# Gated mix of two linear-attention blocks: stationary tiles of 128 columns in M, denominators between output-weight tiles, and A's last output product moved next to B's

## The chip, the cores and the metric

The kernel runs on one core of a Trainium2 chip. A core has five engines that run side by side and wait for one another through semaphores: TensorE (PE, matrix products, with a separate stream of weight loads, PEld), VectorE (DVE), ScalarE (ACT), GpSimd (POOL) and SyncE (SP, which here only issues DMAs). Products land in PSUM, eight banks of 128 partitions by 512 float32; everything else lives in SBUF. The metric is device time in microseconds (us) of one execution; lower is better.

## The reference

Inputs are x (2048 rows of 640), and for each of two branches A and B a weight wqkv (640 by 1920) and wo (640 by 640), all bf16; B's own x is not used. Each branch computes, with 32 heads of 20 columns:

```python
qkv = x @ wqkv                       # q, k, v: 2048 x 640 each
phi = lambda t: jnp.where(t > 0, t + 1, jnp.exp(t)) + 1e-6
pq, pk = phi(q), phi(k)
kv  = einsum("bhsd,bhse->bhde", pk, v)          # 20 x 20 per head
z   = einsum("bhsd->bhd", pk)
o   = einsum("bhqd,bhde->bhqe", pq, kv) / (einsum("bhqd,bhd->bhq", pq, z) + 1e-6)
branch = o @ wo
```

The output is g * A + (1 - g) * B, with one gate per row, g = sigmoid(sum(x * gate_w)).

## The kernel before

The work is reordered so that v is never formed. With pk the 2048 by 640 matrix of k features, G = x^T pk is 640 by 640; M = Wv^T G, of which only the diagonal blocks of the heads are needed, gives kv; WP = blockdiag(kv) wo is then a 640 by 640 weight, and the branch is (pq / den) WP. The order of the work is written out by hand: a small recording layer takes operations in program order, gives each engine its own list, and derives the semaphore waits from the tiles that operations read and write. Every engine runs its list strictly in that order.

The stages, in order of time:

- Transposes of x, the k products of all 16 row tiles of both branches with their feature maps (to about 48 us), then the q products and the G pieces of A mixed (to about 114 us). `g_piece` is one quarter of one 128-row strip of G: four row tiles, each a matmul of 512 and one of 128 moving columns.
- `m_part`: M in ten windows `w` of 80 columns of Wv by 64 columns of G (`W = 80`, `HS` the first head of each window). A window is five accumulating matmuls, stationary `WV[X][:, j, ds]` (128 rows by 80 columns), moving 64 columns of `GT`. Windows 0 to 7 go to one PSUM bank, 8 and 9 to another; VectorE then multiplies rows 0 to 79 by a mask of the head blocks into `MG`. One branch is 50 matmuls; both branches together are 100.
- `wp_tile`: one of five 128-row tiles `k` of WP. Each half (320 columns) is four matmuls that stand side by side in the array, with 32 stationary columns each, writing to partitions 32 g to 32 g + 31. ScalarE copies the first half out of PSUM, VectorE the second. The PSUM pairs of A's five tiles are 1, 2, 3, 1, 2 (pair p is banks 2p and 2p + 1).
- `den`: the denominators of one branch, 20 matmuls of 512 moving columns with 32 stationary columns, four side by side, into bank 6 (A) or 7 (B). VectorE adds EPS (L641), then takes reciprocals in four pieces for each branch (`recip`, L649). SP writes them to DRAM (`table`) and reads them back spread over the partitions (`widen`); VectorE multiplies the q features by them (`scale`, L684 and L692).
- `wp_a_den` issues A's five WP tiles, then A's and B's denominators, then reciprocals, tables and widened reads. It is hung into the G pieces of B: M of A stands after B's first G piece, `wp_a_den` after the second, and the other 18 pieces follow.
- `fin_mm(X, t)`: the output product of row tile t, five matmuls of 512 and five of 128 moving columns. `fin_a(t)` (ScalarE, L779) writes A's product times the gate to the float32 tile `TA[t % 5]`; `fin_out(t)` (VectorE, L796) adds B's product times one minus the gate, into `OSTG`, and a DMA writes it out. A's PSUM pairs are 2 and 1 by turns, B's 0 and 3. Between A's first output tiles stand M and the WP tiles of B.
- The closing loop runs over t = 0 to 15: A's tile t + 3 (for t from 1 to 12), then B's tile t. So the last products are A15, B12, B13, B14, B15. B's last tile is cut in three column pieces, 0 to 255, 256 to 479, 480 to 639, each in its own bank with its own VectorE instruction and its own DMA (ScalarE's queue for the first and third, SP's for the second).

Of the kernel before, what the change touches and what calls it, by code (L numbers as in the profile page):

```python
# [8 lines left out]
ACT = mybir.ActivationFunctionType  # L9
# [3 lines left out]
D = 640  # L13
H = 32
DH = 20
# [13 lines left out]
NW = 10  # L29
W = 80  # L30
HS = (0, 3, 6, 9, 12, 16, 19, 22, 25, 28)

C_MK = 0
C_ZM = 64 * NW
# [171 lines left out]
def bass_gated_mix__linear_attn_block__linear_attn_block__prompt_kernel(  # L206
# [18 lines left out]
    with ExitStack() as es:  # L225
        E = es.enter_context

        def sb(name, shape, dtype=dt.bfloat16):
            return E(nc.sbuf_tensor(name, shape, dtype))
# [7 lines left out]

        WK = {"A": sb("WKA", [128, NC, D]), "B": sb("WKB", [128, NC, D + 2])}
        WQ = {X: sb("WQ" + X, [128, NC, D]) for X in BR}
        WV = {X: sb("WV" + X, [128, NC, D]) for X in BR}  # L240
        PK = {X: sb("PK" + X, [128, NT, D]) for X in BR}
        PQ = {X: sb("PQ" + X, [128, NC, S]) for X in BR}
        WP = {X: sb("WP" + X, [128, NC, D]) for X in BR}
# [25 lines left out]
        def bank(i, lo, hi, p0=0, p1=128):  # L269
            o = 512 * (i % 2)  # L270
            return PP[i // 2][p0:p1, o + lo : o + hi]
# [38 lines left out]
        def act(fn, reads=(), writes=(), name=""):  # L310
            return sch.op("ACT", fn, reads=reads, writes=writes, name=name)
# [4 lines left out]
        def pool(fn, reads=(), writes=(), name=""):  # L316
            return sch.op("POOL", fn, reads=reads, writes=writes, name=name)
# [30 lines left out]
        def load_wk(eng, X, c0, c1):  # L348
# [19 lines left out]
            reads=[("ONE",)],  # L368
            writes=[("IDN",)],
        )  # L370
        act(
            lambda e: e.activation(SG[:, 2, 0:1], nc.const_aps.tensor(1.0, (128, 1), dt.float32), ACT.Exp),
            writes=[("SGE", 0)],
# [252 lines left out]
        def den(X, bk):  # L626
            xi = BR.index(X)
            steps = []
            for k in range(NC):
                for b in range(NB):  # L630
                    o = bank(bk, 0, 512, 32 * b, 32 * b + 32)
                    r = PQ[X][:, k, 512 * b : 512 * b + 512]
                    steps.append((o, ZBD[:, NC * xi + k, :], r, k == 0, k == NC - 1, (0, 32 * b)))
            mms(
                steps,
                reads=[("ZBD", X)] + [("PQ", X, b, k) for k in range(NC) for b in range(NB)],
                writes=[("PS", bk)],
                name="den%s" % X,
            )
            dve(  # L640
                lambda e: e.tensor_scalar(DT32[X][:, :], bank(bk, 0, 512), EPS, None, op0=ALU.add),  # L641
                reads=[("PS", bk)],
                writes=[("DT", X)],
            )
# [53 lines left out]
        def m_part(X, w0, w1, bk):  # L698
            n = w1 - w0
            steps = []  # L700
            for w in range(w0, w1):
                ds = slice(DH * HS[w], DH * HS[w] + W)
                steps += acc(
                    bank(bk, 64 * (w - w0), 64 * (w - w0) + 64, 0, W),
                    [(WV[X][:, j, ds], GT[:, j, 64 * w : 64 * w + 64]) for j in range(NC)],
                )
            mms(
                steps,
                reads=[("WV", X)] + [("GT", j) for j in range(NC)],
                writes=[("PS", bk)],  # L710
                name="m%s%d" % (X, w0),
            )
            dve(
                lambda e: e.tensor_tensor(
                    out=MG[:, w0:w1, :].rearrange("p w f -> p (w f)"),
                    in0=bank(bk, 0, 64 * n, 0, W),
                    in1=CB[0:W, C_MK + 64 * w0 : C_MK + 64 * w1],
                    op=ALU.mult,
                ),
                reads=[("PS", bk), ("CST",)],  # L720
                writes=[("MG", w) for w in range(w0, w1)],
            )

        def wp_tile(X, k, pp):
            P = PP[pp]
            cells = []
            for g in range(4):
                w = 8 + g // 2 if k == 4 else 4 * (k // 2) + g
                fs = slice(32 * (g % 2), 32 * (g % 2) + 32) if k == 4 else slice(k % 2, 64, 2)
                cells.append((w, MG[:, w, fs]))  # L730
            for j, (lo, hi) in enumerate(((0, D // 2), (D // 2, D))):
                mms(
                    [
                        (P[32 * g : 32 * g + 32, 512 * j : 512 * j + hi - lo], l, wo_at(X, w)[0][:, lo:hi], True, True, (0, 32 * g))
                        for g, (w, l) in enumerate(cells)
                    ],
                    reads=[("WO", X, w) for w, _ in cells] + [("MG", w) for w, _ in cells],
                    writes=[("PS", 2 * pp + j)],
                    name="wp%s%d" % (X, k),
                )  # L740
            for j, (lo, hi) in enumerate(((0, D // 2), (D // 2, D))):
                o, p = WP[X][:, k, lo:hi], P[:, 512 * j : 512 * j + hi - lo]
                (dve if j else act)(
                    lambda e, o=o, p=p, j=j: e.tensor_copy(o, p) if j else e.activation(o, p, ACT.Copy),
                    reads=[("PS", 2 * pp + j)],
                    writes=[("WP", X, k, j)],
                )
# [16 lines left out]
        def fin_mm(X, t):  # L764
            for lo, hi, bk in fin_split(X, t):
                mms(
                    acc(
                        bank(bk, 0, hi - lo),
                        [(PQ[X][:, k, 128 * t : 128 * t + 128], WP[X][:, k, lo:hi]) for k in range(NC)],
                    ),  # L770
                    reads=[("PQ", X, t // 4, k) for k in range(NC)] + [("WP", X, k, j) for k in range(NC) for j in (0, 1)],
                    writes=[("PS", bk)],
                    name="fin%s%d" % (X, t),
                )

        def fin_a(t):
            pp = fin_pp("A", t)
            act(
                lambda e: e.activation(TA[:, t % 5, :], PP[pp][:, 0:D], ACT.Copy, scale=SG[:, 0, t : t + 1]),  # L779
                reads=[("PS", 2 * pp), ("PS", 2 * pp + 1), ("SG", "A")],  # L780
                writes=[("TA", t % 5), ("PK", "B", 2 * (t % 5)), ("PK", "B", 2 * (t % 5) + 1)],
            )

        def fin_out(t):
            slot = t % 3
            pp = fin_pp("B", t)
            sem = out_sems[slot]
            last = t == NT - 1
            pieces = (
                [(lo, hi, bank(bk, 0, hi - lo), [bk]) for lo, hi, bk in fin_split("B", t)]  # L790
                if last
                else [(0, D, PP[pp][:, 0:D], [2 * pp, 2 * pp + 1])]
            )
            for i, (lo, hi, p, bks) in enumerate(pieces):
                dve(
                    lambda e, lo=lo, hi=hi, p=p: e.scalar_tensor_tensor(  # L796
                        out=OSTG[:, slot, lo:hi],
                        in0=p,
                        scalar=SG[:, 1, t : t + 1],
                        in1=TA[:, t % 5, lo:hi],  # L800
                        op0=ALU.mult,
                        op1=ALU.add,
                    ),
                    reads=[("TA", t % 5), ("SG", "B")] + [("PS", bk) for bk in bks],
                    writes=[("OSTG", slot, i)],
                )
                out_counts[slot] += 16

                def fn(engobj, lo=lo, hi=hi):
                    return engobj.dma_start(  # L810
                        out[0, 128 * t : 128 * t + 128, lo:hi], OSTG[:, slot, lo:hi]
                    ).then_inc(sem, 16)

                sch.op(
                    "ACT" if last and i != 1 else "SP",
                    fn,
                    reads=[("OSTG", slot, i)],
                    name="out%d" % t,
                    sem=sem,
                    total=out_counts[slot],  # L820
                )
# [51 lines left out]
                mains.append(lambda j=j, q=q: g_piece("B", j, q, j % 2))  # L873

        def wp_a_den():
            for k in range(NC):
                wp_tile("A", k, (1, 2, 3)[k % 3])
            den("A", 6)
            den("B", 7)
            for X in BR:  # L880
                for i in range(4):
                    recip(X, i)
                for b in range(NB):
                    table(X, b)
            for b0, b1 in ((0, 1), (1, NB)):
                for X in BR:
                    widen(X, b0, b1)
# [21 lines left out]
        fin_a(3)  # L909
        later = {1: ("B", 1), 2: ("A", 2), 5: ("B", 2), 6: ("A", 3), 9: ("B", 3)}  # L910
        for t in range(NT):
            if 0 < t < NT - 3:
                fin_mm("A", t + 3)
                fin_a(t + 3)
            fin_mm("B", t)
            fin_out(t)
            if t in later:
                scale(*later[t])
# [39 lines left out]
```

## Time and profile before

| what | us |
|---|---|
| time, median of 3 runs (lowest, highest) | 194.15 (194.10, 194.21) |
| span of the profiled execution, first to last instruction | 191.9 |
| median less that span, what lies around the instructions | 2.25 |
| TensorE busy (98% of the span) | 188.2 |
| VectorE busy (65%) | 124.3 |
| ScalarE busy (39%) | 75.0 |
| GpSimd busy (23%) | 44.5 |

The profile gives the profiled execution's span only; its own time is taken as the span and the 2.25 us around it. TensorE's records are pipelined: the duration of one matmul includes the way through the array, so that successive matmuls overlap in the records. What a matmul costs in a stream is the distance from its start to the next one's start. A merged line of the timeline gives the start of the first instruction, the time from there to the end of the last, and the count; the distance is therefore (length less the duration of one) divided by (count less one). The granted TensorE clock was full in every slice.

### The profile page before, as it was taken

The numbers are of one execution on the slowest core, as the hardware profiler recorded it, in microseconds if no ns is written. First come the engines' busy times: TensorE is split into PE (matmuls) and PEld (weight loads), VectorE is DVE, ScalarE is ACT, GpSimd is POOL, SyncE is SP. The second block draws the span as 40 slices with busy tenths as digits, with TensorE's granted clock in tenths as the row PEclk, the third lists the DMA queues.
The fourth block names the chain that finished last, engine by engine and source line by source line (L and its number), as shares of the span: only waits on it lengthen the run. The fifth ranks groups of instructions, "written<-read, shape, count | busy, mean of one in ns | idle before, by whom it ended". The sixth has DMA issues, their size and how long they took to land.

```text
span 191.9 us, 3569 instructions
## 1 busy us (share of the span) xinstructions
PE 188.2 (98%) x1428; PEld 103.6 (54%) x1428; DVE 124.3 (65%) x211; ACT 75.0 (39%) x130; POOL 44.5 (23%) x36
## 2 busy tenths in 40 slices
PE   7999999999999999999999999999999999999994
PEld 4555555555454444445454557555557555555553
DVE  0298999998996765757676744890422856582544
ACT  3466565565642624444335332122123533223310
POOL 1000223253226566536547410000000000000000
PEclk9999999999999999999999999999999999999999
DMA  5967569993400000011000003038596011111214
GB/s 186 319 119 102 100 104 373 366 352 102 126 3 0 0 3 0 21 43 43 3 0 2 0 25 85 3 67 222 155 254 239 3 68 69 37 68 68 72 38 132
DMA packets 22785, 19.07 MB, mean 99 GB/s; under 512 B 10288, under 2 KB 22000, under 8 KB 22768
## 3 DMA queue, kind: packets, MB, share of 16 engines
q1 hardware_dynamic: 21904, 18.08, 33.4%
q10 hardware_dynamic: 864, 0.76, 1.2%
q8 instruction: 11, 0.18, 0.4%
q14 instruction: 6, 0.05, 0.1%
HBM read 12.94 MB, written 3.93 MB: 88 GB/s over the span
## 4 chain that ended last, share of the span: by engine, by line
PE 96%; DMA 1%; DVE 1%; issue 0%; DVEq 0%
PE ps L301 95%; DMA XN<-in_A_x_dram 1%; PE ps L431 1%; DVE OSTG L796 0%; DVE XT L445 0%; DVEq L928 0%; DVEq L158 0%
## 5 line engine op out<-in xcount | busy, mean ns | idle before, releaser
L525 ACT ACTIVATE EQ<-ps 128x512 bf16<-128x512 f32 x40 | 23.9, 597 | 34.1 <-PE ps L301 34.0
L484 ACT ACTIVATE EK<-ps 128x640 bf16<-128x640 f32 x32 | 22.3, 703 | 16.1 <-PE ps L301 15.2
L530 DVE TENSOR_SCALAR EQ<-EQ 128x512 bf16<-128x512 bf16 x40 | 15.3, 383 | 17.8 <-ACT EQ L525 17.1
L577 POOL TENSOR_TENSOR ZS<-ZS,PKA 128x640 f32<-128x640 f32 x13 | 18.7, 1439 | 27.3 <-DVE PKB L500 12.1
L796 DVE SCALAR_TENSOR_TENSOR OSTG<-ps,SG,PKB 128x640 bf16<-128x640 f32 (+3 forms) x18 | 14.3, 808 | 16.3 <-PE ps L301 16.3
L301 PE MATMUL ps<-PKA,XN 128*128 128x512 bf16 (+1 forms) x160 | 24.8, 299 | 0.0
L301 PE MATMUL ps<-WPA,PQA 128*128 128x512 bf16 (+1 forms) x160 | 24.2, 299 | 0.0
L301 PE MATMUL ps<-WPB,PQB 128*128 128x512 bf16 (+4 forms) x165 | 23.9, 295 | 0.0
L301 PE MATMUL ps<-WKA,XT 128*128 128x512 bf16 (+1 forms) x160 | 23.1, 299 | 0.2
L301 PE MATMUL ps<-XT,WQB 128*128 128x512 bf16 x100 | 23.2, 379 | 0.0
L301 PE MATMUL ps<-XT,WQA 128*128 128x512 bf16 x100 | 23.0, 379 | 0.0
L301 PE MATMUL ps<-WKB,XT 128*128 128x512 bf16 (+1 forms) x160 | 22.5, 299 | 0.0
L779 ACT ACTIVATE PKB<-ps,SG 128x640 f32<-128x640 f32 x16 | 12.7, 795 | 24.9 <-PE ps L301 24.9
L301 PE MATMUL ps<-PKB,XN 128*128 128x512 bf16 (+1 forms) x160 | 22.2, 299 | 0.0
L577 POOL TENSOR_TENSOR ZS<-ZS,PKB 128x640 f32<-128x640 f32 x13 | 19.1, 1469 | 13.5 <-DVE PQB L535 11.0
L301 PEld LDWEIGHTS ps<-PKA,XN 128*128 128x128 bf16 x160 | 13.1, 98 | 11.7
L301 PEld LDWEIGHTS ps<-WPB,PQB 128*128 128x128 bf16 x165 | 13.4, 98 | 8.9
L301 PEld LDWEIGHTS ps<-WPA,PQA 128*128 128x128 bf16 x160 | 12.9, 98 | 9.7
L301 PEld LDWEIGHTS ps<-WKB,XT 128*128 128x128 bf16 x160 | 12.4, 97 | 9.6
L301 PEld LDWEIGHTS ps<-WKA,XT 128*128 128x128 bf16 x160 | 12.3, 98 | 9.7 <-DVE XT L445 0.9
L301 PEld LDWEIGHTS ps<-PKB,XN 128*128 128x128 bf16 x160 | 12.2, 98 | 9.6 <-issue 0.4
L495 DVE TENSOR_SCALAR EK<-EK 128x640 bf16<-128x640 bf16 x32 | 14.6, 456 | 2.6 <-ACT EK L484 2.4
(61 smaller groups left out, 154.2 us busy)
## 6 DMA issues: line engine op xcount, KB each, us to landing
out_dram<-OSTG SPq DMA_DIRECT2D x15, 160.0 KB, 1.8
XN<-in_A_x_dram SPq DMA_DIRECT2D x3, 640.0 KB, 8.8
PKA<-rsA SPq DMA_DIRECT2D x3, 384.0 KB, 4.8
XT<-rsB SPq DMA_DIRECT2D x3, 384.0 KB, 7.3
WKB<-in_B_wqkv_dram SPq DMA_DIRECT2D x1, 800.0 KB, 6.7
WQA<-in_A_wqkv_dram SPq DMA_DIRECT2D x1, 800.0 KB, 5.4
WVA<-in_A_wqkv_dram SPq DMA_DIRECT2D x1, 800.0 KB, 10.6
WQB<-in_B_wqkv_dram SPq DMA_DIRECT2D x1, 800.0 KB, 12.2
```

Source lines behind the costliest of these rows:

```text
L301: ins = pe.matmul(o, l, r, start=st, stop=sp, tile_position=tp)
L431: ins = pe.transpose(dst[:, 128 * i : 128 * i + 128], XN[:, t, 128 * c : 128 * c + 128], IDN[:, :],)
L484: lambda e: e.activation(EK[:, slot, :], P[:, 0:D], ACT.Exp),
L495: lambda e: e.tensor_scalar(EK[:, slot, :], EK[:, slot, :], 1.0, EPS, op0=ALU.min, op1=ALU.add),
L525: lambda e: e.activation(EQ[:, slot, :], bank(bk, 0, 512), ACT.Exp),
L530: lambda e: e.tensor_scalar(EQ[:, slot, :], EQ[:, slot, :], 1.0, EPS, op0=ALU.min, op1=ALU.add),
L577: lambda e: e.tensor_tensor(out=o, in0=a, in1=PK[X][:, t, :], op=ALU.add),
L779: lambda e: e.activation(TA[:, t % 5, :], PP[pp][:, 0:D], ACT.Copy, scale=SG[:, 0, t : t + 1]),
L796: lambda e, lo=lo, hi=hi, p=p: e.scalar_tensor_tensor(out=OSTG[:, slot, lo:hi], in0=p, scalar=SG[:, 1, t : t + 1], in1=TA[:, t % 5, lo:hi] ...
```

## The change

There are three parts.

1. M takes 128 stationary columns for each window instead of 80. The columns past the 80 belong to the next heads, or, in the memory of one partition, to the next 128-row strip of the weight; the last window of the last strip would read past the end, so the weight tile of each branch is 48 columns longer (`PAD`), set to zero by GpSimd at the start. The products fill all 128 partitions of the PSUM bank; VectorE still reads rows 0 to 79.
2. `wp_a_den` issues WP tiles 0 and 1, A's denominators, WP tile 2, B's denominators, WP tiles 3 and 4. The PSUM pairs are 1, 2, 1, 2, 1.
3. A's output product 15 with its ScalarE copy moves from before B12 to between B14 and B15, and the copy is cut in two pieces (columns 0 to 255 and 256 to 639). The first VectorE piece of B15 waits for the first of them only.

```diff
+PAD = DH * HS[-1] + 128 - D
...
-        WV = {X: sb("WV" + X, [128, NC, D]) for X in BR}
+        WVF = {X: sb("WV" + X, [128, NC * D + PAD]) for X in BR}
+        WV = {X: WVF[X][:, 0 : NC * D].rearrange("p (c f) -> p c f", c=NC) for X in BR}
...
+        for X in BR:
+            pool(lambda e, X=X: e.memset(WVF[X][:, NC * D : NC * D + PAD], 0.0), writes=[("WVP", X)])
...
-                ds = slice(DH * HS[w], DH * HS[w] + W)
+                d0 = DH * HS[w]
                 steps += acc(
-                    bank(bk, 64 * (w - w0), 64 * (w - w0) + 64, 0, W),
-                    [(WV[X][:, j, ds], GT[:, j, 64 * w : 64 * w + 64]) for j in range(NC)],
+                    bank(bk, 64 * (w - w0), 64 * (w - w0) + 64),
+                    [
+                        (WVF[X][:, D * j + d0 : D * j + d0 + 128], GT[:, j, 64 * w : 64 * w + 64])
+                        for j in range(NC)
+                    ],
                 )
...
-                reads=[("WV", X)] + [("GT", j) for j in range(NC)],
+                reads=[("WV", X), ("WVP", X)] + [("GT", j) for j in range(NC)],
...
-            act(
-                lambda e: e.activation(TA[:, t % 5, :], PP[pp][:, 0:D], ACT.Copy, scale=SG[:, 0, t : t + 1]),
-                reads=[("PS", 2 * pp), ("PS", 2 * pp + 1), ("SG", "A")],
-                writes=[("TA", t % 5), ("PK", "B", 2 * (t % 5)), ("PK", "B", 2 * (t % 5) + 1)],
-            )
+            cuts = (0, 256, D) if t == NT - 1 else (0, D)
+            for i, (lo, hi) in enumerate(zip(cuts, cuts[1:])):
+                act(
+                    lambda e, lo=lo, hi=hi: e.activation(
+                        TA[:, t % 5, lo:hi], PP[pp][:, lo:hi], ACT.Copy, scale=SG[:, 0, t : t + 1]
+                    ),
+                    reads=[("PS", bk) for bk in (2 * pp, 2 * pp + 1)[: 1 + hi // (D // 2)]] + [("SG", "A")],
+                    writes=[("TA", t % 5, i)]
+                    + [("TA", t % 5, j) for j in (0, 1) if t < NT - 1]
+                    + [("PK", "B", 2 * (t % 5) + j) for j in (0, 1) if t < 5],
+                )
...
-                    reads=[("TA", t % 5), ("SG", "B")] + [("PS", bk) for bk in bks],
+                    reads=[("TA", t % 5, j) for j in (0, 1) if not (last and i == 0 and j)]
+                    + [("SG", "B")]
+                    + [("PS", bk) for bk in bks],
...
-            for k in range(NC):
-                wp_tile("A", k, (1, 2, 3)[k % 3])
+            wp_tile("A", 0, 1)
+            wp_tile("A", 1, 2)
             den("A", 6)
+            wp_tile("A", 2, 1)
             den("B", 7)
+            wp_tile("A", 3, 2)
+            wp_tile("A", 4, 1)
...
-            if 0 < t < NT - 3:
-                fin_mm("A", t + 3)
-                fin_a(t + 3)
+            if 0 < t < NT - 4 or t == NT - 1:
+                a = min(t + 3, NT - 1)
+                fin_mm("A", a)
+                fin_a(a)
```

## The prediction

> **What bounds the kernel now.** I read the page first: the busy shares, then the chain of work that ended last, then the timeline around the three places that the change touches.
>
> ```profile
> PE 188.2 (98%) x1428; PEld 103.6 (54%) x1428; DVE 124.3 (65%) x211; ACT 75.0 (39%) x130; POOL 44.5 (23%) x36
> PE 96%; DMA 1%; DVE 1%; issue 0%; DVEq 0%
> PE ps L301 95%; DMA XN<-in_A_x_dram 1%; PE ps L431 1%; DVE OSTG L796 0%; DVE XT L445 0%; DVEq L928 0%; DVEq L158 0%
> ```
>
> TensorE is 98% busy and carries 96% of the chain. From the fourth microsecond to 189.25 us it runs without a real break. So two things count: the start-to-start distance of its matmuls, and what follows the last of them. VectorE, ScalarE and GpSimd matter only where TensorE waits for them.
>
> ```profile
> 4.74 0.44 PE L431 MATMUL ps<-IDN,XN 128*128 128x128 bf16 x5
> ...
> 115.22 0.28 PE L301 MATMUL ps<-ONE,ZP 128*128 128x32 bf16 x5
> 115.35 2.08 PE L301 MATMUL ps<-GT,WVA 128*80 128x64 bf16 x50
> 117.27 1.25 PE L301 MATMUL ps<-PKB,XN 128*128 128x512 bf16 x8
> ...
> 118.45 0.85 PE L301 MATMUL ps<-WKA,MG 80*32 80x320 bf16 x17
> 119.31 0.09 PEld L301 LDWEIGHTS ps<-WKA,MG 80*32 80x32 bf16 x1 [0.20 <-ACT WPA L744]
> 120.05 1.25 PE L301 MATMUL ps<-PQA,ZBD 128*32 128x512 bf16 x20
> 121.13 1.25 PE L301 MATMUL ps<-PQB,ZBD 128*32 128x512 bf16 x20
> 122.31 0.11 PEld L301 LDWEIGHTS ps<-PKB,XN 128*128 128x128 bf16 x2 [0.42 <-issue]
> ```
>
> These are M of A, its WP tiles and the denominators. M's 50 matmuls take (2.08 - 0.203) / 49 = 38.3 ns each, although 64 moving columns are few. The line above it shows another small product with the full 128 stationary columns: (0.28 - 0.177) / 4 = 26 ns each. In the WP tiles one weight load waits 0.20 us for ScalarE's copy.
>
> ```profile
> L301 PEld LDWEIGHTS ps<-GT,WVA 128*80 128x80 bf16 x50 | 2.0, 121 | 0.0
> L301 PEld LDWEIGHTS ps<-ONE,ZP 128*128 128x128 bf16 x5 | 0.2, 97 | 0.1
> ```
>
> A load of 80 columns takes 121 ns, one of 128 columns 97 ns: the wider is the faster.
>
> ```profile
> 186.65 0.88 DVE L796 SCALAR_TENSOR_TENSOR OSTG<-ps,SG,PKB 128x640 bf16<-128x640 f32 x1 [0.47 <-PE ps L301]
> 188.01 1.93 DVE L796 SCALAR_TENSOR_TENSOR OSTG<-ps,SG,PKB 128x640 bf16<-128x640 f32 x4 [0.47 <-PE ps L301]
> 189.20 0.73 DVE L796 SCALAR_TENSOR_TENSOR OSTG<-ps,SG,PKB 128x224 bf16<-128x224 f32 x2
> 189.32 1.00 ACTq L810 DMA_DIRECT2D out_dram<-OSTG  x2
> ```
>
> This is the end. VectorE runs B14 and the three pieces of B15 without a gap from 188.01 to 189.94, while TensorE is through at 189.25. The last piece (374 ns) starts at 189.56, some 0.3 us after its product was there. Its DMA is issued when it ends and lands at about 191.5.
>
> **Part 1, M.** Removed are 100 matmuls at 38.3 ns, added 100 with 128 stationary and 64 moving columns. No row has that pair, so I bound it. Below: 26 ns, the 128-column row with 32 moving columns, since more moving columns cannot cost less. Above, if width buys nothing: 38.3 ns; rival 1 has what lies beyond. Between them: the five transposes, 128 by 128, stand (0.44 - 0.223) / 4 = 54 ns apart, and the denominators (1.08 us for five rows of 512) 216 ns, so 0.42 ns a moving column and 27 ns for 64. The 32-column row costs more than its columns, so I add a little and take 29 ns, nearer to the 26 ns row because that one shares the stationary shape. The gain is 100 x (38.3 - 29) = 0.93 us, ends 0 and 1.23. All of it is on TensorE's path, half at 115 us, half at 144.6 us.
>
> The Trainium skill, "TensorE: Matmul & The Clock Gate", section "Weight-path perf modes", says that the fast weight load is on when the number of weights is 128 and the type is not float32; by that rule 80 columns miss it, and the trace agrees (121 against 97 ns).
>
> What could be late next: the mask product of VectorE (0.69 us for the first bank, 0.28 for the second), which the WP tiles need. It follows M's own matmuls, and behind M of A stands a G piece of B (117.27 to 118.36) or, for B, output tile A2 (1.36 us). With M shorter, the first mask product ends some 2.1 us after M's start and TensorE reaches the WP tiles 1.45 + 1.09 = 2.54 us after it: covered by 0.4 us, by 0.7 for B. GpSimd's two fills of 48 columns (a 128-column one took 0.20 us) stand behind the identity and before its first addition, which waited 20 us: nothing. No DMA changes size, number or place ahead of these stages.
>
> **Part 2, denominators between WP tiles.** Ten half tiles take (0.85 - 0.30) / 4 = 0.137 us each unhindered (the first line of 17), 1.37 in all; they took 120.05 - 118.45 = 1.60. The 0.23 us lost is TensorE waiting for PSUM, because ScalarE and VectorE copy a half in 0.32 to 0.41 us. In the new order tile 2 follows 1.08 us of denominators. It starts 0.55 + 1.08 = 1.63 us into the block and needs tile 0's copies, done 1.0 us into it (ScalarE from 118.82, VectorE 118.96 to 119.45). VectorE now takes A's EPS addition (0.69) before tile 2's copy, which so ends at about 2.98; tile 4's second half needs it at 3.39. Both are covered, by 0.6 and 0.4 us. Gain 0.23 us; ends 0.23 and -0.1 (rival 2).
>
> VectorE's order also moves the reciprocals, behind which stand the tables, the widened reads on SP and the scaling. B's EPS addition would end 3.9 us into the block, two copies of 0.4 follow, the reciprocals start at 4.6, as before (123.04 - 118.45 = 4.59). The block is 0.23 shorter, so they are 0.23 later against TensorE. A's scaling ended at 138.14 and its first output product started at 141.89: 3.7 us of cover become 3.5. SP was waiting for the reciprocals, so nothing is overtaken there. Nothing on the path.
>
> **Part 3, A15 next to B15.** TensorE's work is the same. VectorE gets B14's 0.88 us one product (1.36 us) earlier, at 186.65 instead of 188.01, and is free when B15's pieces arrive. A first piece can start at about 188.56 (0.14 us after the end of its matmuls, as B14's did), the second at 189.03, the third at 189.03 + 0.36 = 189.39, instead of 189.56; if the second piece is not held, at 189.30. Gain 0.17 to 0.26, taken 0.20; ends 0 and 0.26. The issue and the 1.5 us to landing follow unchanged. ScalarE's copy of A15 (0.80 us whole, some 0.4 and 0.55 in pieces) starts at about 187.65, ends at 188.05 and 188.55; B15's first two pieces ask for them at 188.46 and 188.94. Covered by 0.4 us. SP and ScalarE queues: B14's DMA leaves 1.36 us earlier, its rows are gone sooner, and no issue is overtaken. B11 to B14 now follow each other at 1.36 us with 0.88 us on VectorE; B12, B13, B14 did so before.
>
> **Sum.** 0.93 + 0.23 + 0.20 = 1.36 us. The profiled span is 191.9, with 2.25 around it 194.15, which is also the median; so 194.15 - 1.36 = 192.8 us, 0.7% faster. A measurement here tells 0.2% (0.39 us) from no change.
>
> **Rivals.**
>
> 1. *The wider load costs by its columns* (the other side). Place: M alone. If the load sets the distance in proportion, 38.3 x 128 / 80 = 61 ns, so M costs 2.3 us more, less 0.43 of the other parts: 196.0 us. It decides from 38.3 + 4.3 + 3.9 = 46.5 ns a matmul on. For it: M's loads have M's rhythm, so the load does set the distance now. Against: the 128-column loads at 26 ns. The columns come at offsets of 40 bytes here, which no 128-column row has. The Trainium skill, the same page, section "LDWEIGHTS (loading the stationary operand)", states that a load's time is its columns divided by 1.2; that would be 1.6 times as long for 128 as for 80, and the rows contradict it (97 against 121 ns). 0.07.
> 2. *Changing between WP and denominators drains the array.* Between 128-wide and 32-wide stationary tiles TensorE loses about 0.1 us: the denominators took 122.31 - 120.05 = 2.26 for two times 1.08. If the 80-row WP tiles and the 128-row denominators are also different settings, four changes replace one, 0.3 us more: 193.1. Against: the one such change in the trace came 0.15 us after the last half tile (119.90 to 120.05), hardly above 0.137. The Trainium skill, "TensorEngine Tiling (Array Packing)", section "Key Properties", says that changing the tiling mode drains TensorE, changing the tile does not; by it the sum depends on whether 80 rows count as 128, which the trace suggests. 0.08.
> 3. *The width buys nothing*: M stays at 38 ns because something other than the load sets it: 194.15 - 0.43 = 193.7, at the edge of what can be told. Against: 38.3 is far above both 26 and 27. 0.08.
> 4. *The end does not move*: the third piece starts no sooner, because the second is held or the DMAs set the end: 193.0. 0.07.
>
> **How the numbers follow.** Forecast 192.8 with 0.70; its own range 192.4 to 193.1. The range 192.3 to 193.5 takes in M at 26 ns with the better end (194.15 - 1.23 - 0.23 - 0.26 = 192.4), rivals 2 and 4, alone or together; rivals 1 and 3 (0.15) are left out. Faster: 0.70 + 0.08 + 0.07 + half of rival 3 = 0.89; same 0.04; slower 0.07.
>
> **What would show it.** M's line of 50 matmuls should be about 1.6 us long instead of 2.08, with loads near 97 ns. From the first WP tile to the next G piece it should be about 3.63 us instead of 3.86, with no wait for ScalarE. VectorE should idle between B14 and B15's pieces, the third starting within 0.15 us of TensorE's end. M at 40 ns or more, a WP tile waiting for VectorE's EPS addition, or VectorE waiting for ScalarE at the end would make this wrong.

## The result

The changed kernel takes 192.72 us (median of 5 runs, 192.62 to 193.19), the kernel before beside it 194.10 us (194.03 to 194.21). The ratio is 0.9933, interval 0.9921 to 0.9945: 0.7% faster, 1.38 us. The forecast was 192.8.

The timeline of TensorE in the changed kernel, M of A to the end of the denominators (start, length, engine, line, names, shapes, count):

```profile
115.70 1.62 PE L304 MATMUL ps<-GT,WVA 128*128 128x64 bf16 x50
...
118.34 0.73 PE L304 MATMUL ps<-WKA,MG 80*32 80x320 bf16 x16
118.89 1.25 PE L304 MATMUL ps<-PQA,ZBD 128*32 128x512 bf16 x20
119.97 0.30 PE L304 MATMUL ps<-WKA,MG 80*32 80x320 bf16 x1
...
120.25 1.26 PE L304 MATMUL ps<-PQB,ZBD 128*32 128x512 bf16 x20
121.33 0.30 PE L304 MATMUL ps<-WKA,MG 80*32 80x320 bf16 x1
```

The same for its weight loads:

```profile
118.34 0.39 PEld L304 LDWEIGHTS ps<-WKA,MG 80*32 80x32 bf16 x16 [0.26 <-issue]
...
121.98 0.60 PEld L304 LDWEIGHTS ps<-PKB,XN 128*128 128x128 bf16 x5 [0.27 <-issue]
```

M's 50 matmuls now take 1.62 us; (1.62 - 0.193) / 49 = 29.1 ns each instead of 38.3. M of B does the same: its line is 1.62 us long instead of 2.07. From the first WP tile (118.34) to the next G piece (121.98) it is 3.64 us instead of 3.86. No weight load in between waits for ScalarE any more. From the first half tile to the denominators it is 0.55 us for four halves, the denominators take 1.08, tile 2 takes 0.28, B's denominators 1.08: each piece at its unhindered length, with no loss at the changes between WP tiles and denominators.

The groups of M by shape show the loads (busy us, mean ns of one, idle before):

```profile
L304 PE MATMUL ps<-GT,WVA 128*128 128x64 bf16 x50 | 1.6, 193 | 0.0
L304 PEld LDWEIGHTS ps<-GT,WVA 128*128 128x128 bf16 x50 | 1.5, 98 | 0.0
```

A load of 128 columns takes 98 ns where one of 80 took 121.

The end, in the timelines of VectorE, of ScalarE, and of all engines together (so that the last two of VectorE's pieces appear twice, and the last matmul and ScalarE's DMA issues are seen):

```profile
185.88 0.89 DVE L810 SCALAR_TENSOR_TENSOR OSTG<-ps,SG,PKB 128x640 bf16<-128x640 f32 x1 [0.47 <-PE ps L304]
187.78 1.19 DVE L810 SCALAR_TENSOR_TENSOR OSTG<-ps,SG,PKB 128x256 bf16<-128x256 f32 x3 [1.02 <-PE ps L304]
...
186.94 1.08 ACT L789 ACTIVATE PKB<-ps,SG 128x256 f32<-128x256 f32 x2 [5.72 <-PE ps L304]
...
188.23 0.74 DVE L810 SCALAR_TENSOR_TENSOR OSTG<-ps,SG,PKB 128x224 bf16<-128x224 f32 x2
188.24 0.23 PE L304 MATMUL ps<-WPB,PQB 128*128 128x160 bf16 x1
188.29 1.06 ACTq L826 DMA_DIRECT2D out_dram<-OSTG  x2
```

VectorE now stands idle for 1.02 us between B14 and the pieces of B15, and what it waits for is TensorE. It ends at 188.97, 0.50 us after TensorE's end at 188.47; before, it ended 0.69 us after (189.94 against 189.25).

### Where the spans differ ahead of the change

The spans of the two profiles differ by 0.9 us only (191.9 and 191.0), because M of A starts 0.35 us later in the second. That is the start of the execution: the third row tile of x arrived later. It is not the longer weight tile either, for two more kernels that have it, M at 112 columns and one copy of A15 (both below), transpose this tile at 6.13 and 6.09 us without a wait. TensorE's timeline of the changed kernel, then of the kernel before:

```profile
6.41 0.45 PE L436 MATMUL ps<-IDN,XN 128*128 128x128 bf16 x5 [0.19 <-DMA XN<-in_A_x_dram]
```

```profile
6.07 0.44 PE L431 MATMUL ps<-IDN,XN 128*128 128x128 bf16 x5
```

So I compare profiles by the time from the start of M of A to the end of the span, which leaves the start out: 191.9 - 115.35 = 76.55 us before, 191.0 - 115.70 = 75.30 after, 1.25 us less (rounded to about 0.1).

### The profile page after: what moved, and what is told of

The parts are those of the page before. It is cut to its first block, busy times and chain, and to the rows that moved or that the text cites. A ratio compares the mean times of both kernels' runs of the same rounds, so it can differ in the third digit from the quotient of the medians.

```text
span 191.0 us, 3548 instructions
## 1 busy us (share of the span) xinstructions
PE 185.7 (97%) x1402; PEld 102.7 (54%) x1428; DVE 124.5 (65%) x211; ACT 75.5 (40%) x131; POOL 44.6 (23%) x38
## 4 chain that ended last, share of the span: by engine, by line
PE 90%; DVE 3%; DMA 2%; issue 1%; ACT 1%; SPq 0%; DVEq 0%
PE ps L304 90%; DMA XN<-in_A_x_dram 2%; DVE PKA L505 2%; DVE EK L500 1%; ACT WPB L752 1%; DVE OSTG L810 0%; SPq L293 0%; PE ps L436 0%; DVE PKB L505 0%; ACT EK L489 0%; DVEq L948 0%; DVEq L159 0%
## 5 line engine op out<-in xcount | busy, mean ns | idle before, releaser
L304 PE MATMUL ps<-PKA,XN 128*128 128x128 bf16 (+1 forms) x156 | 24.5, 297 | 0.2
L789 ACT ACTIVATE PKB<-ps,SG 128x640 f32<-128x640 f32 (+2 forms) x17 | 13.0, 764 | 28.7 <-PE ps L304 28.7
L304 PE MATMUL ps<-WPA,PQA 128*128 128x128 bf16 (+1 forms) x155 | 23.3, 297 | 0.4 <-ACT WPB L752 0.2
L304 PE MATMUL ps<-WPB,PQB 128*128 128x128 bf16 (+4 forms) x162 | 23.4, 294 | 0.2
L304 PE MATMUL ps<-WKA,XT 128*128 128x128 bf16 (+1 forms) x157 | 22.7, 298 | 0.4
L304 PE MATMUL ps<-PKB,XN 128*128 128x512 bf16 (+1 forms) x156 | 21.7, 297 | 0.3 <-issue 0.2
L304 PEld LDWEIGHTS ps<-WPB,PQB 128*128 128x128 bf16 x165 | 13.4, 98 | 8.9
```

What stands on the lines that cost most here:

```text
L304: ins = pe.matmul(o, l, r, start=st, stop=sp, tile_position=tp)
L789: lambda e, lo=lo, hi=hi: e.activation(TA[:, t % 5, lo:hi], PP[pp][:, lo:hi], ACT.Copy, scale=SG[:, 0, t : t + 1]),
```

## Experiments

My theory is that of the prediction: three gains that add up, 0.93 on the distance of M's matmuls, 0.23 on the wait for PSUM, 0.20 on VectorE's queue at the end. The rivals are the four given there. Each part was made alone, one was made at another width, and two took away what a gain was put down to. The kernel before was timed beside them, 194.17 us beside the first four and 194.12 us beside the last three.

### Part 1 alone

```diff
-                    bank(bk, 64 * (w - w0), 64 * (w - w0) + 64, 0, W),
-                    [(WV[X][:, j, ds], GT[:, j, 64 * w : 64 * w + 64]) for j in range(NC)],
+                    bank(bk, 64 * (w - w0), 64 * (w - w0) + 64),
+                    [
+                        (WVF[X][:, D * j + d0 : D * j + d0 + 128], GT[:, j, 64 * w : 64 * w + 64])
+                        for j in range(NC)
+                    ],
```

with the longer weight tile as in the change.

> The kernel before with part 1 alone: M with 128 stationary columns; denominators, WP tiles and A15 as before. My theory: 100 matmuls go from 38.3 to 29.2 ns, all of it on TensorE's path, so 0.92 us of 194.1: 193.2 us, and M's line of 50 is 1.62 us long. Rival (the gain of the whole change comes from the order of the work, M's saving is given back as a wait for the masked products): 194.1 us, with an idle stretch before the first WP tile.

Measured: 193.22 us, ratio 0.9956 (0.9942 to 0.9971), 0.95 us less. TensorE's timeline:

```profile
116.03 1.62 PE L304 MATMUL ps<-GT,WVA 128*128 128x64 bf16 x50
117.48 1.25 PE L304 MATMUL ps<-PKB,XN 128*128 128x512 bf16 x8
118.67 0.85 PE L304 MATMUL ps<-WKA,MG 80*32 80x320 bf16 x17
```

M is 1.62 us long. From the start of the G piece to the first WP tile it is 118.67 - 117.48 = 1.19 us, as before (118.45 - 117.27 = 1.18), so nothing was given back as a wait for the masked products. From M's start to the end of the span it is 191.7 - 116.03 = 75.67 us, 0.88 less than before.

### Part 2 alone

The edit is the second part of the diff, on the kernel before.

> The kernel before with part 2 alone: WP tiles 0, 1, denominators A, tile 2, denominators B, tiles 3, 4. My theory: the block from the first WP tile to the next G piece goes from 3.86 to 3.63 us, 193.9 us. Rival (each change between 80-row WP tiles and 128-row denominators drains the array for about 0.1 us): the block stays at 3.9 us, 194.1 to 194.2 us, and the first denominators start 0.24 us after the last half tile instead of 0.14.

Measured: 194.08 us, ratio 0.9990 (0.9977 to 1.0004); the runs alone can't tell it from no change. The loads and, in the last line, TensorE show what it does:

```profile
119.23 0.39 PEld L301 LDWEIGHTS ps<-WKA,MG 80*32 80x32 bf16 x16 [0.26 <-issue]
...
122.87 0.66 PEld L301 LDWEIGHTS ps<-PKB,XN 128*128 128x128 bf16 x6 [0.27 <-issue]
...
119.78 1.25 PE L301 MATMUL ps<-PQA,ZBD 128*32 128x512 bf16 x20
```

The block is 122.87 - 119.23 = 3.64 us, as in the changed kernel, against 3.86. The first denominators start 0.55 us after the first of four halves (119.23 to 119.78), which is 0.137 for each, the unhindered length: no drain there. From M's start to the end it is 192.5 - 116.13 = 76.37 us, 0.18 less. So by the profile the part gains some 0.2 us, 0.1% of the time, which is inside the spread of the runs.

### Part 3 alone

```diff
-            if 0 < t < NT - 3:
-                fin_mm("A", t + 3)
-                fin_a(t + 3)
+            if 0 < t < NT - 4 or t == NT - 1:
+                a = min(t + 3, NT - 1)
+                fin_mm("A", a)
+                fin_a(a)
```

with the copy of A15 in two pieces.

> The kernel before with part 3 alone: A15 between B14 and B15, its copy in two pieces. My theory: the third piece of B15 starts 0.13 us after TensorE's modelled end instead of 0.32, 193.9 us. Rival (the end is set by the DMAs): third piece earlier, but the last landing not, 194.1 us.

Measured: 193.91 us, ratio 0.9986 (0.9971 to 1.0001), 0.26 us less and again at the edge of what the runs can tell. In VectorE's timeline the gap before B15 is there:

```profile
188.63 1.19 DVE L804 SCALAR_TENSOR_TENSOR OSTG<-ps,SG,PKB 128x256 bf16<-128x256 f32 x3 [1.02 <-PE ps L303]
```

VectorE ends at 189.82, TensorE at 189.32 (its last line starts at 187.79 and is 1.53 long): 0.50 us apart as in the changed kernel. From M's start to the end it is 191.8 - 115.43 = 76.37 us, 0.18 less. From VectorE's end to the end of the span it is 1.98 us (before 1.96): the DMAs followed, so they don't hold the end where it was.

### M at 112 columns

```diff
-                    bank(bk, 64 * (w - w0), 64 * (w - w0) + 64),
+                    bank(bk, 64 * (w - w0), 64 * (w - w0) + 64, 0, 112),
...
-                        (WVF[X][:, D * j + d0 : D * j + d0 + 128], GT[:, j, 64 * w : 64 * w + 64])
+                        (WVF[X][:, D * j + d0 : D * j + d0 + 112], GT[:, j, 64 * w : 64 * w + 64])
```

> The whole change, but with 112 stationary columns in M instead of 128; nothing is left out, the products used are the same 80 rows. My theory (the load is fast at exactly 128 columns, and costs by the column otherwise): 38.3 x 112 / 80 = 53.6 ns a matmul, M costs 2.4 us more than with 128, 195.1 us, loads above 121 ns. Rival a (any tile wider than some width is fast): 29 ns, 192.7 us. Rival b (80 columns were slow for a reason other than the load): 38 ns or less, 193.6 us or less.

Measured: 195.05 us, ratio 1.0058 (1.0037 to 1.0078). The groups of M, and TensorE's timeline:

```profile
L304 PE MATMUL ps<-GT,WVA 128*112 128x64 bf16 x50 | 2.7, 216 | 0.0
L304 PEld LDWEIGHTS ps<-GT,WVA 128*112 128x112 bf16 x50 | 2.7, 132 | 0.0
...
115.37 2.75 PE L304 MATMUL ps<-GT,WVA 128*112 128x64 bf16 x50
```

The distance is (2.75 - 0.216) / 49 = 51.7 ns, a load 132 ns. From 80 to 112 columns that is 13.4 ns more, 0.42 ns a column, with about 4.8 ns that don't depend on the width. So rival 1 was right about these two widths: a matmul costs by the stationary column, a little less than in proportion (51.7 against 53.6 expected). By that line 128 columns would have cost 58 ns; they cost 29. Rival b falls, and rival a falls for every threshold up to 112 columns. Widths between 112 and 128 were not tried, so that the tile must have exactly 128 columns is likely but not shown. The records of the loads move the same way (121, 132 and 98 ns for 80, 112 and 128 columns), which speaks for the load as the cause; but the partitions that a product fills grow with the columns here, and no run parts the two.

### Two PSUM pairs with nothing between

```diff
-            wp_tile("A", 0, 1)
-            wp_tile("A", 1, 2)
+            for k in range(NC):
+                wp_tile("A", k, (1, 2)[k % 2])
             den("A", 6)
-            wp_tile("A", 2, 1)
             den("B", 7)
-            wp_tile("A", 3, 2)
-            wp_tile("A", 4, 1)
```

> The whole change, but WP tiles of A on pairs 1, 2, 1, 2, 1 with both denominators behind them: two pairs and nothing in between. My theory (TensorE waits in the WP tiles for the copies out of PSUM, 0.44 to 0.49 us each and 0.32 to 0.41 apart): tile 2 waits for tile 0's copies, tile 3 for tile 1's, tile 4 for tile 2's; the WP part takes 2.1 us instead of 1.37, the block from the first WP tile to the next G piece about 4.35 instead of 3.65, so 0.7 us more than the changed kernel: 193.4 us. Rival (what part 2 saves is not the wait for PSUM but a better sequence of array settings): the block as before the change, 3.86 us, 192.9 us.

Measured: 193.52 us, ratio 0.9966 (0.9949 to 0.9983), 0.9 us more than the changed kernel beside it (192.62). The timelines of the weight loads and, in the last line, of TensorE:

```profile
118.55 0.39 PEld L304 LDWEIGHTS ps<-WKA,MG 80*32 80x32 bf16 x16 [0.26 <-issue]
119.48 0.09 PEld L304 LDWEIGHTS ps<-WKA,MG 80*32 80x32 bf16 x1 [0.53 <-issue]
...
120.01 0.09 PEld L304 LDWEIGHTS ps<-WKA,MG 80*32 80x32 bf16 x1 [0.16 <-DVE WPA L752]
...
120.43 0.23 PEld L304 LDWEIGHTS ps<-WKB,MG 80*32 80x32 bf16 x8 [0.32 <-issue]
...
123.00 0.39 PEld L304 LDWEIGHTS ps<-PKB,XN 128*128 128x128 bf16 x4 [0.42 <-issue]
...
119.51 0.30 PE L304 MATMUL ps<-WKA,MG 80*32 80x320 bf16 x1 [0.23 <-ACT WPA L752]
```

The block is 123.00 - 118.55 = 4.45 us, 0.8 more than with the denominators in between. The weight loads of tiles 2, 3 and 4 each stand waiting (0.53, 0.16 and 0.32 us). The first wait is put down to "issue", but the last line, the first matmul of the same tile, names ScalarE's copy (0.23 us); the second names VectorE's; for tile 4 the profile names none. The order of the array settings is that of the kernel before, and yet the block is not the 3.86 us that the rival asks for. So what part 2 saves is the wait for the copies out of PSUM, and the denominators are what covers it.

### A15's copy in one piece

```diff
-            cuts = (0, 256, D) if t == NT - 1 else (0, D)
+            cuts = (0, D)
...
-                    + [("TA", t % 5, j) for j in (0, 1) if t < NT - 1]
+                    + [("TA", t % 5, j) for j in (0, 1)]
...
-                    reads=[("TA", t % 5, j) for j in (0, 1) if not (last and i == 0 and j)]
+                    reads=[("TA", t % 5, j) for j in (0, 1)]
```

> The whole change, but A15's copy in one piece of 640 columns, which B15's first piece waits for. My theory: the copy starts when both banks of A15 are done and ends about 0.3 us after B15's first product is there, so the first piece starts some 0.25 us later and the third about 0.18 us later than in the changed kernel: the gain of part 3 is gone, 192.9 us. Rival (the second and third pieces have slack): the third piece starts where it does in the changed kernel, 192.7 us.

Measured: 193.02 us, ratio 0.9947 (0.9928 to 0.9965), 0.4 us more than the changed kernel beside it, with intervals that overlap. The timelines of VectorE and ScalarE:

```profile
187.67 1.14 DVE L810 SCALAR_TENSOR_TENSOR OSTG<-ps,SG,PKB 128x256 bf16<-128x256 f32 x3 [1.28 <-ACT PKB L789]
...
186.84 0.79 ACT L789 ACTIVATE PKB<-ps,SG 128x640 f32<-128x640 f32 x1 [6.00 <-PE ps L304]
```

B15's first piece now waits for ScalarE, which ends at 187.63; VectorE ends at 188.81, 0.71 us after TensorE's end at 188.10 (its last line starts at 186.78 and is 1.32 long). That is the 0.69 us of the kernel before: without the cut, A15's late place gains nothing.

### The changed kernel once more

> The changed kernel itself, beside the two others on one chip: 192.7 us by the first measurement. Its profile is a second one of the same program: everything behind the first transposes should stand at the same distances as in the first profile, and what differs should lie ahead of them.

Measured: 192.62 us, ratio 0.9922 (0.9901 to 0.9943). TensorE's timeline:

```profile
115.48 1.62 PE L304 MATMUL ps<-GT,WVA 128*128 128x64 bf16 x50
...
118.12 0.73 PE L304 MATMUL ps<-WKA,MG 80*32 80x320 bf16 x16
118.67 1.25 PE L304 MATMUL ps<-PQA,ZBD 128*32 128x512 bf16 x20
```

From M's start to the first WP tile it is 2.64 us in both profiles, to the denominators 3.19. M starts 0.22 us earlier in the execution than in the first profile, and the span is 190.7: the two differ ahead of M.

All profiles by the time from the start of M of A to the end of the span:

| kernel | us | against before | median of its runs |
|---|---|---|---|
| before | 76.55 | | 194.10, 194.17, 194.12 |
| part 1 alone | 75.67 | -0.88 | 193.22 |
| part 2 alone | 76.37 | -0.18 | 194.08 |
| part 3 alone | 76.37 | -0.18 | 193.91 |
| changed, first profile | 75.30 | -1.25 | 192.72 |
| changed, second profile | 75.22 | -1.33 | 192.62 |
| M at 112 columns | 77.53 | +0.98 | 195.05 |
| two pairs (192.0 less 115.92) | 76.08 | -0.47 | 193.52 |
| one copy (190.8 less 115.33) | 75.47 | -1.08 | 193.02 |

The three parts alone add up to 1.24 us, the whole to 1.25 and 1.33; since spans are given to 0.1 us, that is agreement. The runs say a little more, 1.38 and 1.50 us; the rest would lie ahead of M or in the spread, which nothing here separates.

## Why the prediction was right

- *Part 1*: taken 29 ns, measured 29.1; taken 0.93 us, measured 0.88 by the profile and 0.95 by the runs. The row that decided it was the small product with 128 stationary columns, and the loads that were shorter for 128 than for 80 columns. The 2 ns added to the 27 that the moving columns cost came from no row, and the reason given for leaning towards 26 (the same stationary shape) holds for the transposes at 54 ns too; that the guess fitted to 0.1 ns is luck. The covers held: the WP tiles waited no longer for the mask product than before. In the changed kernel VectorE's two mask products end 2.26 us after M's start (its line starts at 117.07 and is 0.89 long) and TensorE reaches the WP tiles 2.64 us after it; the prediction had 2.54, because it counted the G piece as 1.09 us where the profile of before already has 1.18 to the next tile (118.45 - 117.27).
- *Part 2*: taken 0.23, measured 0.22 in the block (3.86 to 3.64). The wait was the one named, as the kernel with two pairs shows. That kernel's own wait was put at 0.7 us and measured 0.8. The cover was sized well: in the changed kernel tile 2's copy on VectorE ends 2.95 us into the block (its line starts at 120.81 and is 0.48 long), where the prediction had 2.98, and the reciprocals start 4.62 us into it.
- *Part 3*: taken 0.20, between 0.17 (the second piece holds the third) and 0.26 (it doesn't). Measured 0.19, from VectorE's end against TensorE's. The second piece does hold the third: VectorE ends at 188.97 and the third takes 0.37, so it starts at 188.60, 0.13 us after TensorE's end and straight behind the second. What was sized badly is the cover of A15's copy: I gave it 0.4 us, but ScalarE's two pieces end at 188.02 and B15's second piece starts at 188.23, so 0.2 us are left: the pieces take 1.08 us together where the prediction had 0.95, and start somewhat later. The one-piece kernel shows that all of the gain hangs on the cut.
- *Rivals*: a wider tile costs by its columns from 80 to 112, but not at 128 (rival 1); changing between 80-row and 128-row tiles of 32 columns costs nothing that the rows show (rival 2); the width buys something (rival 3); the end moves (rival 4).
- *How near the time came* is partly luck. The terms read from the profiles are 0.91 (two lines of M), 0.22 and 0.19, together 1.32 us against 1.36; that the first measurement gave 1.38 lies inside the spread, and the second gave 1.50.
- *The sum's base was wrong without harm.* I took 2.25 us around the span from the median. Wherever an execution's own time and span are both listed it is 1.7 to 1.8 us: 192.72 with a span of 191.0, 192.48 with 190.7, 194.21 with 192.5 for part 2 alone. The profiled execution of before so took about 193.6 us, half a microsecond less than its median. The forecast was a difference to the median and none of its terms lies in the start, so it came out; a sum built up from the span alone would have been 0.5 us off.

## What to carry to other kernels

When a stream of small matmuls is slower than its moving columns, look at the weight loads: if their distance follows the stationary width, a tile filled up to all 128 columns with columns that nobody reads can be cheaper than a narrower one, while padding to fewer can make it dearer (112 columns here). When TensorE waits for PSUM to be copied out, work of the same tiling with its own bank, put between the tiles, covers the wait; count the copies' queue to see how much is needed. At the end of a kernel, look at what the last engine still has in its queue, and cut the operand that arrives last so that the first piece doesn't wait for all of it.

## What was not expected of the hardware

The start of the execution moves by more than two of the three parts are worth. The second group of transposes stands (0.44 - 0.223) / 4 = 54 ns apart in the profile of before. TensorE's timeline for part 2 alone, whose edit stands far behind, with the first two of the group by themselves in the last line:

```profile
4.64 0.72 PE L301 MATMUL ps<-WKA,XT 128*128 128x512 bf16 x2
5.15 0.74 PE L431 MATMUL ps<-IDN,XN 128*128 128x128 bf16 x5
...
5.15 0.42 PE L431 MATMUL ps<-IDN,XN 128*128 128x128 bf16 x2
```

The same five matmuls take 0.74 us from the first start to the last end instead of 0.44, which is (0.74 - 0.42) / 3 = 107 ns apart, and M of A starts at 116.13 instead of 115.35. The granted clock reads 1.00 for the first 6 us of that profile all the same. The Trainium skill, "TensorE: Matmul & The Clock Gate", section 'Part 1: The HAM clock gate (the "warmup" mystery)', says that TensorE starts at half its clock and leaves that at the end of a free-running window, so that the moment varies from run to run. The distances here, 107 and 54 ns, agree with half the clock by that rule, but no run tested it. In the first profile of the changed kernel this group is fast (0.45 us), and what delays M is the late third x tile. In the nine profiles M of A starts between 115.33 and 116.13 us, and runs of one kernel spread by up to 1.1 us (193.68 to 194.82 for the kernel before); that the start makes all of this spread is not shown. Parts of 0.2 us could be shown only by distances inside the profiles.
